# Down, output, key, query and value products as four 32-column strips in one PSUM bank, laid beside the value products of attention

## The chip, the cores and the metric

One core of one Trainium2 chip. The metric is device time in microseconds; every run told of here was in the fast state. The kernel before: 843.19 us, median of 3 runs (843.08 to 843.36). TensorE is called PE here, VectorE DVE and ScalarE ACT, as in the profile.

## The reference, cut to what matters

For 2048 rows of width 512 it adds an attention of 32 heads of 16 to a gated feed-forward of width 1792, with a gate of its own for each row.

```python
q, k, v = qkv[0], qkv[1], qkv[2]                     # x @ wqkv, 32 heads of 16
scores = jnp.einsum("bhqd,bhkd->bhqk", q, k) * (Dh ** -0.5)
p = _softmax(scores, axis=-1)
o = jnp.einsum("bhqk,bhkd->bhqd", p, v)
a = o.transpose(...).reshape(B, S, D) @ wo
b = (_silu(x @ w_gate) * (x @ w_up)) @ w_down
return g * a + (1 - g) * b                           # g = sigmoid(sum(x * gate_w))
```

The softmax has 32 x 2048 x 2048 exponentials: that is the kernel's work. The products are small beside it.

## The kernel before

The program is laid out by a plan that runs when it is built. The plan keeps a foreseen time for PE, DVE and ACT and decides which instruction goes next on each engine. Each turn of the main loop emits a pair of score matmuls (tile s_t, an exponential on ACT follows) and fills PE's room before the next pair with one of: a score block d_t for DVE's own exponential, a value product of attention (o_ps, "pv"), or a piece of side work. DVE's exponentials come in units of four d_t blocks. Side work and d_t share three PSUM banks (`m_tile` takes one, `m_free` gives it back). PE has three forms of instruction: "R", two 64-row halves side by side; "C", four 32-column strips; "F", the full array. The plan counts 0.1 us for each change of form.

Down and output products use `two_banks`: two products run at once in the two row halves, each half adds into its own bank, and after half of the steps they swap halves.

```python
    def two_banks(n, name, a, b, end, stop=True):

        st = {}

        def pc(k):
            v, i = divmod(k, n)

            def f():
                if k == 0:
                    while m_ready(2) is None:
                        stuck()
                    st["a"], st["b"] = m_tile(name + "_a"), m_tile(name + "_b")
                if k == n:
                    sync(ordered(nc.tensor.nop()), st["half"])
                    spend("R", 0.1 if st["seq"] < plan.seq else 1.5)
                for ps, (w, r), h in ((st["a"], a(i), v), (st["b"], b(i), 1 - v)):
                    rows = slice(64 * h, 64 * h + 64)
                    st["half"] = mm(ps[:, :], lhsT=w[rows, :], rhs=r[rows, :], start=(k == i == 0),
                                    stop=(stop and k == 2 * n - 1), tile_position=(64 * h, 0), skip_group_check=True)
                spend("R", 1)
                st["seq"] = plan.seq
                if k == 2 * n - 1:
                    end(st["a"], st["b"])
            return f
        return [(1, pc(k), 2 if k == 0 else 0, "R", st if k == n else None) for k in range(2 * n)]
```

Key, query and value products are in the full form, two steps a piece:

```python
    def k_pieces(b, tb):

        st = {}

        def pc(h):
            def f():
                if h == 0:
                    st["p"] = m_tile("kp")
                    if tb == 0:


                        kst[b] = (on_t[1], bblk)[b == 1][:, :, :].rearrange("p b q -> p (b q)")
                for dc in (2 * h, 2 * h + 1):
                    mm(st["p"][:, :], lhsT=wqk[:, dc, D + P * b:D + P * (b + 1)],
                       rhs=xT[:, dc, tb * QBW:(tb + 1) * QBW], start=(dc == 0), stop=(dc == DC - 1))
                spend("F", 2)
                if h == 1:
                    later(0.6, lambda: end(tb, st["p"]))
            return f
        # ... end(): copy to SBUF, free the bank
        return [(2, pc(0), True), (2, pc(1), False)]

    def down_pieces(qb, tq):

        def rows(t):
            return lambda fc: (mt[:, fc, t * P:(t + 1) * P], wd_t[:, fc, :])

        def done_down(pa, pb):
            for t, p in ((tq, pa), (tq + 1, pb)):
                later(0.65, lambda t=t, p=p: end(t, p))
        # ... end(t, p): scale into bblk, free the bank
        return two_banks(FC, "dps", rows(tq), rows(tq + 1), done_down)
```

The choice in the main loop:

```python
            n_pv = pv_list(plan.pe)
            switch = 0.0 if plan.mode == "C" else 0.1
            fits = int((room + SLACK - switch) / 0.216)
            c = side(room + SLACK)
            if n_pv and fits > 0 and (plan.mode == "C" or len(n_pv) > 1 and fits > 1 and (pv_turn[0] or c is None)
                                      or back >= EB - 4 or c is None and fits == 1):
                emit_pv(n_pv[0])
                pv_turn[0] = False
                continue
            if c is not None:
                put_piece(c)
                pv_turn[0] = True
                continue
            # ... keep-busy strips, or the next pair of scores
```

## Time and profile before

| | before |
|---|---|
| time | 843.19 us |
| ACT busy | 97%: 850 exponentials e_t of 1024 columns, 56 tanh |
| DVE busy | 93%: 87 units of exponentials (348 blocks d_t), all evictions |
| PE matmuls | 5987, changes of form 1052 (counted in the trace) |
| DVE idle, 25 to 820 us | 36.4 us |

The prediction below shows the page's lines, the table of windows, DVE's waits and two pieces of PE's timeline. One habit is needed for all that follows: an ACT instruction that starts late shows as a longer step from start to start, not always as idle time, because two e_t overlap. So I use a ledger: first e_t + 0.904 us for each further e_t + 26.7 us of tanh + a rest = start of the last e_t; after it comes the tail.

### The profile page before, as it was taken

The page shows a single profiled execution, that of the slowest core. Times are in us where ns is not written, and L with a number is a line of the kernel's source. Part 1 is how long each engine was busy: PE and PEld are TensorE (multiplying, and loading weights), DVE is VectorE, ACT ScalarE, POOL GpSimd, SP SyncE. Part 2 cuts the span into 40 slices and gives each one's busy share as a digit, 9 for nine tenths or more (in the row PEclk, how much of TensorE's full clock was granted, in tenths as well). Part 3 has the DMA queues.
Part 4 walks back from the last instruction along what each step waited for, and adds up shares of the span by engine and source line. Part 5 has one row for each costly group of instructions (what it writes and reads, how often), then busy time and mean ns, then how long its engine had stood idle before and what let it go on. Part 6 is the DMA issues. An engine that isn't in the chain of part 4 may idle for free. (4 is left out here: it accounts for less than half of the span.)

```text
span 840.3 us, 16080 instructions
## 1 busy us (share of the span) xinstructions
PE 759.7 (90%) x5987; PEld 260.4 (31%) x6020; DVE 785.5 (93%) x1141; ACT 815.2 (97%) x916; POOL 94.9 (11%) x120
## 2 busy tenths in 40 slices
PE   7899899899989999999899998898999988998986
PEld 3222232233333333233333332222333322332322
DVE  6999998989999989999999899989999999999895
ACT  3999999999999999999999999999999999999996
POOL 5010100100101011110111101010011011000110
PEclk9999999999999999999999999999999999999999
DMA  9432252544455433554445435453544445363240
GB/s 204 128 70 45 57 98 58 108 92 86 96 104 111 92 80 73 108 114 92 99 88 107 80 87 105 92 107 74 104 90 80 91 95 108 89 124 60 58 95 26
DMA packets 101127, 77.18 MB, mean 92 GB/s; under 512 B 77728, under 2 KB 89592, under 8 KB 101048
## 3 DMA queue, kind: packets, MB, share of 16 engines
q0 software_dynamic: 12384, 45.09, 28.7%
q1 hardware_dynamic: 86792, 30.60, 15.5%
q8 instruction: 47, 0.77, 0.4%
q10 hardware_dynamic: 1872, 0.46, 0.2%
q14 instruction: 32, 0.26, 0.1%
HBM read 20.83 MB, written 2.34 MB: 28 GB/s over the span
## 5 line engine op out<-in xcount | busy, mean ns | idle before, releaser
L160 ACT ACTIVATE e_t<-s_t 128x1024 bf16<-128x1024 f32 x850 | 797.0, 1173 | 5.3 <-PE s_t L157 5.2
L157 PE MATMUL s_t<-qx,kaug 64*128 64x512 bf16 x1376 | 279.3, 380 | 51.0 <-ACT e_t L160 44.6
L157 PEld LDWEIGHTS <-kaug 64*128 64x128 bf16 x2048 | 140.3, 93 | 341.4 <-issue 306.5
L166 DVE TENSOR_SCALAR y_t<-d_t 128x512 uint16<-128x512 f32 x348 | 229.0, 682 | 17.9 <-PE d_t L157 15.1
L157 PE MATMUL o_ps<-e_t,vaug 128*32 128x512 bf16 x1700 | 160.0, 389 | 3.0 <-DVE osb L166 2.9
L157 PE MATMUL gu_b<-xT,wu 64*128 64x512 bf16 x440 | 133.1, 375 | 0.4 <-DVE y_t L166 0.2
L157 PE MATMUL gu_a<-xT,wg 64*128 64x512 bf16 x440 | 132.4, 375 | 0.0
L157 PE MATMUL d_t<-qx,kaug 64*128 64x512 bf16 x288 | 105.3, 377 | 4.6 <-DVE y_t L166 1.6
L157 PEld LDWEIGHTS <-vaug 128*32 128x32 bf16 (+1 forms) x2084 | 44.8, 94 | 139.0 <-issue 138.1
L802 POOL DMA_DIRECT2D y_t<-u_t x43 | 40.5, 943 | 356.2 <-PE s_t L157 165.6
L802 POOL DMA_DIRECT2D y_t<-kaug x36 | 36.6, 1016 | 294.8 <-PE s_t L157 141.3
L157 PE MATMUL dps_b<-wd_t,mt 64*128 64x512 bf16 x224 | 65.6, 375 | 0.0
L157 PE MATMUL dps_a<-wd_t,mt 64*128 64x512 bf16 x224 | 65.3, 375 | 0.0
L166 DVE TENSOR_SCALAR z_t<-y_t 128x2048 uint16<-128x2048 uint16 x87 | 60.1, 691 | 2.1
L166 DVE TENSOR_SCALAR y_t<-y_t 128x2048 uint16<-128x2048 uint16 x87 | 59.5, 684 | 1.4 <-DMA y_t<-kaug 1.4
L166 DVE TENSOR_TENSOR u_t<-u_t 128x2048 f16<-128x2048 f16 x43 | 52.6, 1223 | 1.1
L166 DVE TENSOR_TENSOR u_t<-u_t,z_t 128x2048 f16<-128x2048 f16 x43 | 52.3, 1216 | 0.0
L157 PE MATMUL s_t<-q,kaug 64*128 64x512 bf16 x216 | 43.8, 386 | 4.7 <-ACT e_t L160 4.0
L166 DVE TENSOR_TENSOR kaug<-kaug 128x2048 f16<-128x2048 f16 x37 | 45.2, 1222 | 0.9
L157 PEld LDWEIGHTS <-wg 64*128 64x128 bf16 (+1 forms) x444 | 41.2, 94 | 15.6 <-issue 1.8
L157 PEld LDWEIGHTS <-wu 64*128 64x128 bf16 (+1 forms) x444 | 41.3, 94 | 12.7 <-issue 0.9
L166 DVE TENSOR_TENSOR kaug<-kaug,z_t 128x2048 f16<-128x2048 f16 x37 | 45.0, 1215 | 0.0
(136 smaller groups left out, 631.0 us busy)
## 6 DMA issues: line engine op xcount, KB each, us to landing
y_t<-u_t POOLq DMA_DIRECT2D x43, 512.0 KB, 4.9
y_t<-kaug POOLq DMA_DIRECT2D x36, 512.0 KB, 4.9
wg<-in_B_w_gate_dram SPq DMA_DIRECT2D x56, 128.0 KB
wu<-in_B_w_up_dram SPq DMA_DIRECT2D x56, 128.0 KB
y_t<-wd_t POOLq DMA_DIRECT2D x7, 512.0 KB, 4.6
on<-osb SPq DMA_DIRECT2D x120, 16.0 KB
rb<-rr SPq DMA_DIRECT2D x15, 128.0 KB
wd_t<-in_B_w_down_dram SPq DMA_DIRECT2D x7, 256.0 KB
```

The source lines that it names most:

```text
L157: return ordered(nc.tensor.matmul(*args, **kw))
L160: ordered(nc.scalar.activation(*args, **kw))
L166: return lambda *a, **kw: ordered(f(*a, **kw))
L802: nc.gpsimd.dma_start(out=ya, in_=ua, accum_op=ALU.add)
```

## The change

The intent: make the side products in the form of the value products of attention, so that they can lie next to them with no change of form between, and make each in one bank.

```diff
+    def columns(n, name, lhs, rhs, end, c0=0):
+        st = {}
+        def pc(k):
+            def f():
+                if k == 0:
+                    st["p"] = m_tile(name)
+                w, r = lhs(k), rhs(k)
+                for j in range(4):
+                    mm(st["p"][32 * j:32 * j + 32, c0:QBW], lhsT=w[:, 32 * j:32 * j + 32], rhs=r, start=(k == 0),
+                       stop=(k == n - 1), tile_position=(0, 32 * j), skip_group_check=True)
+                spend("C", 1)
+                if k == n - 1:
+                    end(st["p"])
+            return f
+        return [(1, pc(k), k == 0) for k in range(n)]
 # k_pieces, v_pieces, q_pieces, q0_pieces, lone gate and up chains: (cut)
-        return [(2, pc(0), True), (2, pc(1), False)]
+        return columns(DC, "kp", lhs, ..., lambda p: later(0.6, lambda: end(tb, p)))
 # down and output, now one tile of rows a chain: (cut)
-        return two_banks(FC, "dps", rows(tq), rows(tq + 1), done_down)
+        return columns(FC, "dps", ..., lambda p: later(0.65, lambda: end(p)))
-        for tq in range(0, TQ, 2):
+        for tq in range(TQ):
 # planned DVE durations: value copy 0.7 -> 0.54, reciprocal 1.0 -> 0.87,
 # normalisation 0.45 -> 0.345, key maximum 2.6 -> 2.46
-            soon = [c for c in ready if len(c.pieces[c.i]) == 3 and c.deadline <= plan.slot + 4]
-            if len(cur.pieces[cur.i]) > 3 and soon:
+            soon = [c for c in ready if len(c.pieces) <= DC and c.deadline <= plan.slot + 4]
+            if len(cur.pieces) > DC and soon:
-            if n_pv and fits > 0 and (plan.mode == "C" or len(n_pv) > 1 and fits > 1 and (pv_turn[0] or c is None)
-                                      or back >= EB - 4 or c is None and fits == 1):
+            col = c is not None and (c.pieces[c.i][3:] or "C")[0] == "C"
+            visit = len(n_pv) + (len(c.pieces) - c.i if col else 0)
+            if n_pv and fits > 0 and (plan.mode == "C" or visit > 1 and fits > 1 and (pv_turn[0] or c is None or col)
+                                      or back >= EB - 4 or (c is None or col) and fits == 1):
```

`soon` lets a short chain that is almost due interrupt a longer one; `visit` counts the value products and strip steps that could share one change of form.

More of the change, by code (lines that the diff above doesn't have):

```diff
@@ L407, in k_pieces @@
     def k_pieces(b, tb):
-        st = {}
-        def pc(h):
-            def f():
-                if h == 0:
-                    st["p"] = m_tile("kp")
-                    if tb == 0:
-                        kst[b] = (on_t[1], bblk)[b == 1][:, :, :].rearrange("p b q -> p (b q)")
-                for dc in (2 * h, 2 * h + 1):
-                    mm(st["p"][:, :], lhsT=wqk[:, dc, D + P * b:D + P * (b + 1)],
-                       rhs=xT[:, dc, tb * QBW:(tb + 1) * QBW], start=(dc == 0), stop=(dc == DC - 1))
-                spend("F", 2)
-                if h == 1:
-                    later(0.6, lambda: end(tb, st["p"]))
-            return f
         def end(t, p):
@@ L435, in end, with lhs @@
                                           in_=kst[b][DH * hh:DH * (hh + 1), :])
-        return [(2, pc(0), True), (2, pc(1), False)]
+        def lhs(dc):
+            if dc == 0 and tb == 0:
+                kst[b] = (on_t[1], bblk)[b == 1][:, :, :].rearrange("p b q -> p (b q)")
+            return wqk[:, dc, D + P * b:D + P * (b + 1)]
+        return columns(DC, "kp", lhs, lambda dc: xT[:, dc, tb * QBW:(tb + 1) * QBW],
+                       lambda p: later(0.6, lambda: end(tb, p)))
     def k_bound(b):
@@ L454, in v_pieces, with end @@
     def v_pieces(tt):
-        st = {}
-        def pc(h):
-            def f():
-                if h == 0:
-                    st["p"] = m_tile("vp")
-                for dc in (2 * h, 2 * h + 1):
-                    mm(st["p"][:, 64:D], lhsT=xT[:, dc, tt * P:(tt + 1) * P], rhs=wv[:, dc, 64:D],
-                       start=(dc == 0), stop=(dc == DC - 1))
-                spend("F", 2)
-                if h == 1:
-                    later(0.7, end)
-            return f
-        def end():
+        def end(p):
             dst = vaug[:, tt, 4 * VC:G * 4 * VC].rearrange("p (h c) -> p h c", c=VC)[:, :, 1:1 + DH]
-            vec.tensor_copy(out=dst, in_=st["p"][:, 64:D].rearrange("p (h c) -> p h c", c=DH))
-            m_free(st["p"], plan.dve)
-        return [(2, pc(0), True), (2, pc(1), False)]
+            vec.tensor_copy(out=dst, in_=p[:, 64:D].rearrange("p (h c) -> p h c", c=DH))
+            m_free(p, plan.dve)
+        return columns(DC, "vp", lambda dc: xT[:, dc, tt * P:(tt + 1) * P], lambda dc: wv[:, dc, 64:D],
+                       lambda p: later(0.54, lambda: end(p)), c0=64)
     qx = [big.tile([P, 2, 2, QBW], BF16, name=f"qx{i}") for i in range(2)]
@@ L492, in q_pieces, with landed, end @@
     def q_pieces(qb, b):
-        st = {}
-        def pc(h):
-            def f():
-                if h == 0:
-                    st["p"] = m_tile("qp")
-                for dc in (2 * h, 2 * h + 1):
-                    mm(st["p"][:, :], lhsT=wqk[:, dc, P * b:P * (b + 1)],
-                       rhs=xT[:, dc, qb * QBW:(qb + 1) * QBW], start=(dc == 0), stop=(dc == DC - 1))
-                spend("F", 2)
-                if h == 1:
-                    st["c"] = plan.chain
-                    later(0.6, end, key=("q", b))
-            return f
-        def end():
-            me = st["c"]
+        def landed(p):
+            me = plan.chain
+            later(0.6, lambda: end(p, me), key=("q", b))
+        def end(p, me):
             qst = work.tile([P, QBW], BF16, tag="qst", name="qst")
-            vec.tensor_copy(out=qst[:, :], in_=st["p"][:, :])
-            m_free(st["p"], plan.dve)
+            vec.tensor_copy(out=qst[:, :], in_=p[:, :])
+            m_free(p, plan.dve)
             for hh in range(8):
@@ L525, in end @@
             later(0.21, mag, plan.dve, ("q", b))
-        return [(2, pc(0), True), (2, pc(1), False)]
+        return columns(DC, "qp", lambda dc: wqk[:, dc, P * b:P * (b + 1)],
+                       lambda dc: xT[:, dc, qb * QBW:(qb + 1) * QBW], landed)
     def q0_pieces(qb):
         st = {}
-        def pc(h):
-            def f():
-                if h == 0:
-                    st["p"] = m_tile("qp")
-                for dc in (2 * h, 2 * h + 1):
-                    mm(st["p"][:, :], lhsT=wpad[0][:, dc, :], rhs=xT[:, dc, qb * QBW:(qb + 1) * QBW],
-                       start=(dc == 0), stop=(dc == DC - 1))
-                spend("F", 2)
-                if h == 1:
-                    later(1.2, end)
-            return f
-        def end():
+        def end(p):
             for v in range(2):
-                vec.tensor_scalar(out=q0[qb][:, v, :], in0=st["p"][:, :], scalar1=vsel[:, v:v + 1], scalar2=None,
+                vec.tensor_scalar(out=q0[qb][:, v, :], in0=p[:, :], scalar1=vsel[:, v:v + 1], scalar2=None,
                                   op0=ALU.mult)
-            m_free(st["p"], plan.dve)
+            m_free(p, plan.dve)
             aq = mt[:, 4:6, :]
@@ L553, in end, with end_b @@
             st["aq"] = aq
-        def bound():
-            st["b"] = m_tile("bp")
+        def end_b(p):
             for v in range(2):
-                mm(st["b"][:, :], lhsT=kneg0, rhs=st["aq"][:, v, :], start=(v == 0), stop=(v == 1))
-            spend("F", 2)
-            later(1.2, end_b)
-        def end_b():
-            for v in range(2):
-                vec.scalar_tensor_tensor(out=q0[qb][:, v, :], in0=st["b"][:, :], scalar=vsel[:, v:v + 1],
+                vec.scalar_tensor_tensor(out=q0[qb][:, v, :], in0=p[:, :], scalar=vsel[:, v:v + 1],
                                          in1=q0[qb][:, v, :], op0=ALU.mult, op1=ALU.add)
-            m_free(st["b"], plan.dve)
-        return [(2, pc(0), True), (2, pc(1), False)], [(2, bound, True)]
+            m_free(p, plan.dve)
+        return (columns(DC, "qp", lambda dc: wpad[0][:, dc, :], lambda dc: xT[:, dc, qb * QBW:(qb + 1) * QBW],
+                        lambda p: later(1.2, lambda: end(p))),
+                columns(2, "bp", lambda v: kneg0, lambda v: st["aq"][:, v, :], lambda p: later(1.2, lambda: end_b(p))))
     def bound_pieces(qb, b):
@@ L574, in f @@
             st["p"] = m_tile("bp")
-            mm(st["p"][0:8, :], lhsT=kneg[:, b, :], rhs=aqs[(qb, b)][:, :], start=True, stop=True)
-            spend("F", 1)
+            mm(st["p"][0:8, :], lhsT=kneg[:, b, :], rhs=aqs[(qb, b)][:, :], start=True, stop=True,
+               tile_position=(0, 0))
+            spend("C", 1)
             later(0.6, end)
@@ L605, in f @@
             later(0.15, end)
-        return [(0.7, f, True)]
+        return [(0.7, f, True, "F", None)]
     def gate_end():
@@ L658, in gu_chain, with end @@
             return two_banks(DC, "gu", rows(w_gate, i), rows(w_up, i - 1), both)
-        st = {}
         get, end = (rows(w_gate, 0), gate) if i == 0 else (rows(w_up, i - 1), lambda p: later(0.6, lambda: gated(p)))
-        def pc(h):
-            def f():
-                if h == 0:
-                    st["p"] = m_tile("gu")
-                for dc in (2 * h, 2 * h + 1):
-                    w, r = get(dc)
-                    mm(st["p"][:, :], lhsT=w, rhs=r, start=(dc == 0), stop=(dc == DC - 1))
-                spend("F", 2)
-                if h == 1:
-                    end(st["p"])
-            return f
-        return [(2, pc(0), True), (2, pc(1), False)]
+        return columns(DC, "gu", lambda dc: get(dc)[0], lambda dc: get(dc)[1], end)
     scaled = set()
     def down_pieces(qb, tq):
-        def rows(t):
-            return lambda fc: (mt[:, fc, t * P:(t + 1) * P], wd_t[:, fc, :])
-        def done_down(pa, pb):
-            for t, p in ((tq, pa), (tq + 1, pb)):
-                later(0.65, lambda t=t, p=p: end(t, p))
-        def end(t, p):
-            n = qb * TQ + t
+        def end(p):
+            t, n = tq, qb * TQ + tq
             share = omg if qb < QB - 1 else ge
@@ L693, in end @@
             m_free(p, plan.dve)
-        return two_banks(FC, "dps", rows(tq), rows(tq + 1), done_down)
+        return columns(FC, "dps", lambda fc: mt[:, fc, tq * P:(tq + 1) * P], lambda fc: wd_t[:, fc, :],
+                       lambda p: later(0.65, lambda: end(p)))
     e_of = {}
@@ L927, in spread @@
                                   in_=rr[8 * b:8 * b + 8, :].unsqueeze(1).broadcast_to([8, DH, QBW]))
-        at.setdefault(n0 + 6, []).append(lambda: later(1.0, spread))
+        at.setdefault(n0 + 6, []).append(lambda: later(0.87, spread))
         for b in range(g1 // 2):
@@ L932, in norm @@
                 normed.add((qb, b))
-            at.setdefault(n0 + 13 + b, []).append(lambda norm=norm: later(0.45, norm))
+            at.setdefault(n0 + 13 + b, []).append(lambda norm=norm: later(0.345, norm))
     def recip_here(osb):
@@ L978, in fin_pieces, with end @@
     def fin_pieces(qb, tq):
-        def rows(t):
-            return lambda b: (onc[qb][:, b, t * P:(t + 1) * P], wo_t[:, b, :])
-        def done_fin(pa, pb):
-            for t, p in ((tq, pa), (tq + 1, pb)):
-                later(0.67, lambda t=t, p=p: end(t, p))
-        def end(tq, p):
+        def end(p):
             store(qb * TQ + tq, p, bblk[:, tq, :])
             m_free(p, plan.dve)
-        return two_banks(NB, "a_ps", rows(tq), rows(tq + 1), done_fin)
+        return columns(NB, "a_ps", lambda b: onc[qb][:, b, tq * P:(tq + 1) * P], lambda b: wo_t[:, b, :],
+                       lambda p: later(0.67, lambda: end(p)))
     kp0 = [ps_s.tile([P, 2 * QBW], F32, tag="s", name="kp0") for _ in range(2)]
@@ L1092, in bnd @@
                 def bnd(b=b):
-                    later(2.6, lambda: k_bound(b))
+                    later(2.46, lambda: k_bound(b))
                 after = prev = [pace.add([(0.2, bnd, False)], 0, d - 34, ks)]
@@ L1129 @@
             prev = [c]
-        for tq in range(0, TQ, 2):
-            c = pace.add(down_pieces(qb, tq), 0 if qb else 100, a0 + per * (0.6 + 0.3 * (tq + 2) / TQ if qb < QB - 1 else 0.68 + 0.32 * (tq + 2) / TQ), prev + fin_prev + gates)
+        for tq in range(TQ):
+            c = pace.add(down_pieces(qb, tq), 0 if qb else 100, a0 + per * (0.6 + 0.3 * (tq + 1) / TQ if qb < QB - 1 else 0.68 + 0.32 * (tq + 1) / TQ), prev + fin_prev + gates)
             prev = [c]
@@ L1140 @@
             break
-        for tq in range(0, TQ, 2):
+        for tq in range(TQ):
             rel = (UNIT.index((qb, G - 1)) + 1) * KT + 24
-            dl = max(a0 + per * (0.9 + 0.1 * (tq + 2) / TQ), rel + 7 + 3 * tq)
+            dl = max(a0 + per * (0.9 + 0.1 * (tq + 1) / TQ), rel + 7 + 3 * tq)
             def cond(qb=qb):
@@ L1245, in side @@
         mms, _, takes = c.pieces[c.i][:3]
-        mode, two = c.pieces[c.i][3:] or ("F", None)
+        mode, two = c.pieces[c.i][3:] or ("C", None)
         if two and two["seq"] == plan.seq:
```

## The prediction

> **What bounds the kernel now.** I read the head of the page first, then the costliest groups.
>
> ```profile
> PE 759.7 (90%) x5987; PEld 260.4 (31%) x6020; DVE 785.5 (93%) x1141; ACT 815.2 (97%) x916; POOL 94.9 (11%) x120
> ...
> L160 ACT ACTIVATE e_t<-s_t 128x1024 bf16<-128x1024 f32 x850 | 797.0, 1173 | 5.3 <-PE s_t L157 5.2
> ...
> L166 DVE TENSOR_SCALAR y_t<-d_t 128x512 uint16<-128x512 f32 x348 | 229.0, 682 | 17.9 <-PE d_t L157 15.1
> ```
>
> The softmax exponentials are shared out. ScalarE (ACT) takes 850 tiles e_t of 1024 columns, VectorE (DVE) makes the rest by arithmetic, 348 blocks d_t of 512 columns in 87 units of four. ACT waits 5.2 us for a score in the whole run. Since two e_t overlap in the pipeline I also took the starts of successive ACT instructions from the timeline: the median from one e_t to the next is 0.904 us. The ledger up to the start of the last e_t, at 830.6 us: first e_t at 18.7, 849 x 0.904 = 767.5, 56 tanh that together hold ACT for 26.7, and 17.7 left over, of which about 13 are in 66 gaps of 0.96 us or more. After the last start come 9.7 us of tail. So **ACT is the bound, and almost all of the time is the number of e_t.** A change on TensorE (PE) can pay in two ways only: the 13 us of late scores, or units that move from ACT to DVE. One unit moved is two e_t fewer, 1.81 us. On DVE it costs 4 x 0.60 (d_t blocks) + 0.72 + 0.73 + 1.14 + 1.18 + 0.60, start to start in the timeline: 6.8 us. So 1 us of free DVE time is worth 0.27 us of ACT.
>
> Next I looked at who lets DVE idle, and in which stretch. This is the table of windows (us, then busy time of each engine with its instructions); 220 to 260 us is gate and up products, 120 to 200 holds key, query and value products, the others hold the down products.
>
> ```profile
> core 0: us, PE busy (x) PEld busy (x) DVE busy (x) ACT busy (x) POOL busy (x), PEclk, DMA share, GB/s
> 120.00:200.00 80.00, 72.80 (x551) 23.74 (x558) 70.56 (x107) 78.08 (x89) 7.46 (x8) 0.98 0.43 86
> 220.00:260.00 40.00, 36.55 (x297) 12.78 (x296) 39.79 (x58) 40.00 (x48) 3.67 (x5) 1.00 0.53 99
> 280.00:320.00 40.00, 38.35 (x338) 14.69 (x338) 37.21 (x51) 40.00 (x45) 3.75 (x4) 1.00 0.37 76
> 460.00:500.00 40.00, 38.92 (x339) 14.10 (x338) 36.43 (x51) 40.00 (x46) 3.45 (x4) 1.00 0.40 87
> 620.00:660.00 40.00, 38.85 (x336) 14.37 (x333) 38.13 (x52) 40.00 (x46) 4.92 (x5) 1.00 0.34 69
> 780.00:820.00 40.00, 37.19 (x325) 13.17 (x323) 36.31 (x53) 39.61 (x44) 3.75 (x4) 1.00 0.36 74
> ```
>
> DVE is idle 0.2 us in the stretch of gate and up, but 9.4 us in 120 to 200 and 2.8 + 3.6 + 1.9 + 3.7 = 12.0 us in the four of down. The waits of DVE name the releaser:
>
> ```profile
> DVE y_t L166 <- PE d_t L157: 15.1, 22, 1.5
> DVE osb L166 <- PE o_ps L157: 5.9, 3, 5.2
> DVE qst L166 <- PE qp L157: 3.3, 3, 1.6
> ```
>
> Last, PE's timeline where key products run, then where down products run.
>
> ```profile
> 188.37 0.39 PE L157 MATMUL s_t<-qx,kaug 64*128 64x512 bf16 x2
> 188.69 0.61 PE L157 MATMUL kp<-xT,wqk 128*128 128x512 bf16 x2
> 189.29 0.39 PE L157 MATMUL s_t<-qx,kaug 64*128 64x512 bf16 x2
> 189.61 0.40 PE L157 MATMUL o_ps<-e_t,vaug 128*32 128x512 bf16 x4
> 190.20 0.39 PE L157 MATMUL s_t<-qx,kaug 64*128 64x512 bf16 x2 [0.19 <-ACT e_t L160]
> ```
>
> ```profile
> 630.37 0.38 PE L157 MATMUL dps_a<-wd_t,mt 64*128 64x512 bf16 x1
> 630.39 0.38 PE L157 MATMUL dps_b<-wd_t,mt 64*128 64x512 bf16 x1
> ...
> 630.65 0.39 PE L157 MATMUL s_t<-qx,kaug 64*128 64x512 bf16 x2
> ...
> 630.97 0.62 PE L157 MATMUL o_ps<-e_t,vaug 128*32 128x512 bf16 x8
> ```
>
> There are three forms: two 64-row halves side by side (scores, gate and up, down), full 128x128 (key, query, value), and four 32-column strips (value products of attention). A step within a form takes 215 to 227 ns. From scores to full is 308 ns and back 366, from scores to strips 306 and back 357 (medians of the starts). A visit away from the scores so costs about 0.23 us for nothing. I counted 1052 changes of form, 232 of them into or out of the full form.
>
> **What the Trainium skill says.** "TensorEngine Tiling (Array Packing)", Tiling Modes, Key Properties: changing the tiling mode drains the engine, changing the tile alone does not. The trace agrees: 91 to 139 ns more at each change. The same page, Restrictions and Gotchas, Gotcha 1: different row tiles may not be in one PSUM bank at once. That is why down now holds dps_a and dps_b together, two of the three side banks that d_t also needs. "TensorE: Matmul & The Clock Gate", Weight-path perf modes, gives the fast weight load to full 128-column weights only, so strips lose it. The trace shows no price here: a 32-column load takes 94 ns against 97 for a 128-column one, and strip steps follow at 226 and then 216 ns with four loads each. "Perfetto Trace Analysis", Identifying the Most-Contended Engine: occupancy is a fair measure for ScalarE and VectorE, not for PE. So I take ACT's 97% seriously and PE's 90% not.
>
> **The change, part by part.**
>
> 1. Instructions. Counted from the program: down 448 matmuls become 896, output 96 become 192, value 64 and key 64 become 256 each, query 76 become 304, its group-0 bound 6 become 24, the two lone gate and up chains 8 become 32: about 1200 more matmuls and as many loads. Array time does not change: a step of four strips is 0.216 us, as two halves or one full product. All four strips read the same moving tile. The keep-busy strips on xT do this already: four start within 10 ns and the next group comes 209 ns after the last. Cost: 0.
>
> 2. Changes of form. Some 110 visits in the full form go (gates and a few singles stay). 110 x 0.23 = 25 us of PE. Where the new strips do not find a value product to lie beside they need a visit of their own, and down, which now sits among scores with no change at all, needs one too. Down and output are 272 steps; with two steps a visit that is some 140 visits, most of them beside one of the 410 visits that exist. I take 50 new ones, 11 us. Net about 14 us of PE, some 150 changes fewer. None of it is on the path while ACT is fed, apart from the late scores: of their 13 us about 3.5 lie between 100 and 140 us, among key and value products. I credit 1 us.
>
> 3. Banks. Down holds one bank for 14 steps in place of two for 28, so its bank-time halves, and two banks stay for d_t. DVE's idle time in the stretches with rewritten products is 9.4 + 12.0 us, and about 3 more round the output products. I let half of these 24 us be won: 12 us.
>
> 4. Planned durations. The order of instructions is fixed by a plan made ahead, which gives DVE a unit when it foresees time for it. The change lowers four planned costs: 16 x 0.16 + 4 x 0.13 + 15 x 0.105 + 4 x 0.14 = 5.2 us. The trace confirms the new values (0.534 for the value copy, 0.860, 0.334, 2.32 + 0.14), so DVE does nothing faster. The plan only stops leaving 5 us unused.
>
> Sum: 12 + 5.2 = 17 us of DVE for more units, 17 / 6.8 = 2.5, times 1.81 = 4.5 us; with 1 us of late scores, 5.5. Half of a unit is not to be had, and tail and head stay, so I take 5: **843.2 - 5 = 838.2 us.**
>
> **The rivals.** (a) Nothing moves: the count of units hangs on where each unit of work ends in the plan, and DVE's waits may come from PE being full, not from banks. For it: PE is 97% busy in 460 to 500 us. Against: the plan gets 5 us of DVE for certain. Then one unit at most, 841 to 843. (b) New visits hurt: down needs strips where no value product is ready, a visit of value product and two strips is 0.65 + 0.2 plus the score's 0.22, over the 0.904 that ACT leaves, and scores come late. If 60 of the 272 steps cost 0.05 us each, 3 us are lost: 842 to 845. Against: two score buffers, and PE idles 67 us between 25 and 820. (c) Nearly all large DVE gaps close, 27 us over 0.15 us in that stretch, and with the 5 that is nearly five units, 9 us: 834.
>
> **Range and chances.** The central case is two to three units. One unit gives about 841, five 833.5. Neither an unchanged time nor a small loss is excluded. 833 to 842.5 should hold it 8 in 10. Faster by over 2% needs 826, nine units, 61 us of DVE where only 36 are idle in the steady part: 0.02. Slower by over 2% would need a mistake in the plan's order: 0.01.
>
> **What would show it.** Right: e_t falls from 850 to 844 or 846, d_t rises from 348 to 356 or 360, PE has some 7200 matmuls, changes of form fall to about 900 with the full ones nearly gone, strip steps stay at 0.216 us, DVE's wait for d_t falls from 15.1 below 9, and its idle time in the down stretches about halves. Wrong: strip steps over 0.23 us, an e_t count of 850, more gaps over 0.96 us between e_t, or DVE idle at the same places with another releaser.

## The result, and the profile after

836.26 us, median of 4 runs (835.1 to 836.42), against 843.28 us for the kernel before, median of 4 (843.08 to 845.26). The ratio is 0.9909, 95% interval 0.9891 to 0.9926. A ratio is the mean time of one kernel's fast runs over that of the other's of the same rounds, so not quite the ratio of the medians. The class is "same" at the 2% mark, and the gain is real.

The page of the kernel after, the same three lines as the prediction shows of the kernel before:

```profile
PE 776.7 (93%) x7230; PEld 248.0 (30%) x7230; DVE 799.5 (96%) x1168; ACT 810.2 (97%) x910; POOL 102.5 (12%) x123
...
L160 ACT ACTIVATE e_t<-s_t 128x1024 bf16<-128x1024 f32 x844 | 791.7, 1165 | 2.4 <-PE s_t L157 2.2
...
L166 DVE TENSOR_SCALAR y_t<-d_t 128x512 uint16<-128x512 f32 x360 | 233.5, 683 | 1.3 <-PE d_t L157 0.8
```

Three units moved from ACT to DVE (850 to 844 e_t, 348 to 360 d_t), and DVE went from 93 to 96%. DVE's waits (us in total, times, longest) show what gave it the time:

```profile
DVE osb L166 <- PE o_ps L157: 5.1, 2, 2.7
DVE o_t L166 <- PE a_ps L157: 3.9, 3, 2.2
...
DVE y_t L166 <- PE d_t L157: 0.8, 2, 0.5
```

The wait for d_t fell from 15.1 to 0.8 us. The down products begin earlier now, so here is the table of windows of the kernel after over its own four stretches of down (columns as in the prediction):

```profile
254.00:301.00 47.00, 46.19 (x477) 12.59 (x473) 46.37 (x64) 46.98 (x52) 7.89 (x7) 1.00 0.37 74
416.00:466.00 50.00, 49.70 (x514) 13.89 (x506) 49.42 (x70) 50.00 (x56) 7.45 (x7) 1.00 0.36 70
597.00:646.00 49.00, 48.38 (x507) 13.62 (x505) 48.55 (x69) 49.00 (x55) 8.71 (x7) 1.00 0.40 78
766.00:811.00 45.00, 43.41 (x463) 12.24 (x455) 44.48 (x66) 44.88 (x50) 5.11 (x5) 1.00 0.40 83
```

DVE is idle 0.63 + 0.58 + 0.45 + 0.52 = 2.2 us there. In the kernel before it was 10.7 us over its own four (288 to 318, 454 to 488, 626 to 657, 779 to 816 us). PE's timeline shows how strips lie beside the value products:

```profile
98.46 0.40 PE L157 MATMUL o_ps<-e_t,vaug 128*32 128x512 bf16 x4
98.69 0.36 PE L157 MATMUL vp<-rb,xT 128*32 128x448 bf16 x4
98.99 0.39 PE L157 MATMUL s_t<-on,kaug 64*128 64x512 bf16 x2
```

The value projection vp follows the attention product 0.23 us later, the step within a form. Where the kernel before made two visits, with four changes of form, this is one. Yet the changes of form as a whole rose from 1052 to 1279. Those with the full form fell from 232 to 22, as foreseen. But visits for strips rose from 410 to 629, since down and output, which lay among the scores at no cost, now need visits.

The ledger of the two profiled runs, worked out from the starts in the timeline (us):

| | first e_t | 0.904 each | tanh | rest | last e_t | tail | span |
|---|---|---|---|---|---|---|---|
| before | 18.7 | 767.5 | 26.7 | 17.6 | 830.6 | 9.7 | 840.3 |
| after | 19.4 | 762.1 | 26.7 | 15.2 | 823.5 | 11.0 | 834.5 |

5.4 of the 5.8 us between these two runs are the six e_t, 2.4 are scores that come less late, and 2.0 were given back at the start and in the tail.

One thing in the traces must be read beside all this: the granted clock of PE. In the profiled run of the kernel before it is 0.50 for 3.4 us, and in that of the kernel after it is nowhere below 1.00 between 5 and 834 us. The table of windows of the kernel before, that stretch and the 3.4 us ahead of it, then such a pair of the run kqv_full, told of below (PEclk is the third figure from the end):

```profile
126.80:130.20 3.40, 1.97 (x14) 0.49 (x10) 2.43 (x5) 2.70 (x3) 0.86 (x1) 1.00 0.04 7
130.20:133.60 3.40, 3.40 (x14) 0.61 (x13) 1.88 (x4) 2.43 (x3) 0.00 (x0) 0.50 0.84 164
```

```profile
106.40:109.80 3.40, 1.42 (x20) 0.45 (x19) 2.70 (x5) 1.18 (x2) 0.00 (x0) 1.00 0.96 184
109.80:113.20 3.40, 3.40 (x24) 0.61 (x16) 3.37 (x5) 2.61 (x4) 0.00 (x0) 0.50 0.16 28
```

Scores come 2.2 us late in 130 to 134 us alone, so most of the 2.4 us of less late scores are this one stretch. The profiled runs of nine of the fourteen kernels have such stretches before the tail, twelve in all. Each follows 3.4 us in which PE was busy only 19 to 70%, but 56% in the run kqv_alone was followed by none. It matters for the size of the gain too. Beside the experiments the kernel before ran 44 times: the 21 runs with a mean clock of 0.996 or more have a median of 841.7 us, the 18 with 0.994 or less 844.0 us. The four runs of the kernel after had 0.996 to 1.000; the clocks of the four runs of the kernel before that they are compared with are not on record. Against 841.7 us, an estimate of the gain at like clocks is 5.4 us of the 7.0.

### The profile page after: what moved, and what is told of

It reads as the page before. It is cut to its first block, busy times and chain, and to the rows that moved or that the text cites. A ratio compares the mean times of both kernels' runs of the same rounds, so it can differ in the third digit from the quotient of the medians.

```text
span 834.5 us, 18549 instructions
## 1 busy us (share of the span) xinstructions
PE 776.7 (93%) x7230; PEld 248.0 (30%) x7230; DVE 799.5 (96%) x1168; ACT 810.2 (97%) x910; POOL 102.5 (12%) x123
## 5 line engine op out<-in xcount | busy, mean ns | idle before, releaser
L166 DVE TENSOR_SCALAR y_t<-d_t 128x512 uint16<-128x512 f32 x360 | 233.5, 683 | 1.3 <-PE d_t L157 0.8
L157 PEld LDWEIGHTS <-kaug 64*128 64x128 bf16 x2048 | 126.0, 93 | 332.4 <-issue 308.6
L157 PE MATMUL o_ps<-e_t,vaug 128*32 128x512 bf16 x1688 | 167.2, 390 | 2.1 <-DVE osb L166 1.4
L749 POOL DMA_DIRECT2D y_t<-u_t x44 | 46.1, 1047 | 369.7 <-PE s_t L157 217.8
L157 PEld LDWEIGHTS <-vaug 128*32 128x32 bf16 (+1 forms) x2096 | 49.1, 93 | 140.4 <-issue 139.3
L157 PE MATMUL dps<-wd_t,mt 128*32 128x512 bf16 x896 | 77.4, 383 | 0.4 <-DVE bblk L166 0.3
L166 DVE TENSOR_TENSOR u_t<-u_t 128x2048 f16<-128x2048 f16 x45 | 55.0, 1222 | 1.0
L166 DVE TENSOR_TENSOR u_t<-u_t,z_t 128x2048 f16<-128x2048 f16 x45 | 54.8, 1218 | 0.2
L160 ACT ACTIVATE th<-gu_a 128x512 bf16<-128x512 f32 x55 | 41.9, 763 | 0.0
```

Source lines behind the costliest of these rows:

```text
L157: return ordered(nc.tensor.matmul(*args, **kw))
L160: ordered(nc.scalar.activation(*args, **kw))
L166: return lambda *a, **kw: ordered(f(*a, **kw))
L749: nc.gpsimd.dma_start(out=ya, in_=ua, accum_op=ALU.add)
```

## The experiments

Theory (**banks**): DVE gets more units because down and output hold one side bank, not two, so d_t blocks find a bank. Rival (**forms**): what pays is the full-form visits of key, query and value that are gone. Second rival (**durations**): the corrected planned durations do it alone. A third, which was not tested by a run of its own, is the **clock**: stretches of PE at half clock that come or stay away. Twelve kernels ran, in three calls, each on one chip with its own runs of the kernel before; 5 rounds each, all correct. A figure in us that is worked out from two ratios is their difference times 843; it compares runs on different chips, and where the medians in us say something else, both are given. "Idle" is DVE's idle time from 25 to 820 us, "rest" and "tail" are of the ledger of the profiled run.

| label | ratio to before (95%) | e_t | idle | rest | tail |
|---|---|---|---|---|---|
| before | 1 | 850 | 36.4 | 17.6 | 9.7 |
| after | 0.9909 (0.9891 to 0.9926) | 844 | 19.2 | 15.2 | 11.0 |
| down_rows | 0.9931 (0.9918 to 0.9944) | 848 | 30.0 | 14.5 | 9.6 |
| hold2 | 0.9966 (0.9952 to 0.9981) | 850 | 36.3 | 14.0 | 9.6 |
| down_full | 0.9924 (0.9907 to 0.9940) | 846 | 24.6 | 13.7 | 10.2 |
| old_place | 0.9934 (0.9921 to 0.9947) | 844 | 19.2 | 18.2 | 9.5 |
| bank_only | 1.0029 (1.0010 to 1.0048) | 846 | 27.4 | 17.7 | 16.5 |
| consts_only | 0.9994 (0.9972 to 1.0016) | 850 | 37.6 | 16.6 | 9.7 |
| old_consts | 0.9938 (0.9916 to 0.9959) | 848 | 30.4 | 16.6 | 9.5 |
| kqv_full | 1.0083 (1.0060 to 1.0106) | 846 | 32.7 | 23.7 | 16.3 |
| kqv_alone | 0.9953 (0.9936 to 0.9970) | 850 | 37.1 | 14.2 | 9.6 |
| late_ffn | 0.9999 (0.9981 to 1.0017) | 844 | 21.7 | 19.2 | 13.0 |
| gu_cols2 | 0.9916 (0.9893 to 0.9939) | 842 | 14.2 | 15.9 | 13.6 |
| nopre2 | 0.9892 (0.9869 to 0.9915) | 842 | 12.3 | 16.4 | 10.1 |

### down_rows: down and output back in two banks

```diff
 # in the kernel after
-        return columns(FC, "dps", ...)      # and the output products
+        return two_banks(FC, "dps", rows(tq), rows(tq + 1), done_down)
```

> The kernel after, but with the down and output products as before: two of them at a time in 64-row halves, two banks held for 28 steps. Key, query, value in strips, planned durations and placement as changed. Bank theory (the gain is DVE getting d_t blocks because down and output hold one bank and not two): most of the gain goes, the program as built has 848 e_t and 352 d_t (88 units, two fewer than 90), so 3.6 us slower than the kernel after, 839 to 841; DVE idle in the down stretches comes back to about 12 us, in 120 to 200 us it stays under 3. Form theory (the gain is the full-form visits of key, query and value that are gone): the gain stays, 836 to 837, since those are still strips.

Measured 836.41 us against 841.86 for before on that chip, ratio 0.9931. Both theories were too sure: in us the form theory's 836 to 837 was met, by the ratio the run lies between the two, and its interval overlaps that of the kernel after. DVE's idle time in the down stretches came back (15.6 us over 255 to 287, 416 to 451, 593 to 627 and 760 to 814 us) and two units were lost, as banks say. But 5.8 us of the gain stayed (0.0069 of 843), and the one unit that is left is 1.8 of them, so something else pays too, which banks did not foresee; kqv_alone below looks at it alone.

### hold2: strips, but a second bank is held and not used

```diff
+                if two and "h" not in st:        # two=True for down and output
+                    t = m_ready()
+                    if t is not None and t <= plan.pe:
+                        st["h"] = min((i for i in range(3) if banks[i] is not None), key=lambda i: banks[i])
+                        banks[st["h"]] = None
```

> The kernel after with one thing undone: each down and output chain takes a second side bank in the plan, as soon as one is free, and leaves it unused until it ends. Same matmuls, same strips. Bank theory: the gain of this part goes, the program as built has 850 e_t and 348 d_t, so 840 to 843. Form theory: strips are as before, changes of form stay at about 1270 against 1279, so 836 to 837.

Ratio 0.9966: 4.8 us slower than the kernel after by the ratios (0.0057 of 843), 2.6 us by the medians (838.9 against 836.26), with the same strips and 1277 changes of form against 1279. Three units were lost. The first two down stretches of hold2 in the table of windows:

```profile
253.00:296.00 43.00, 42.76 (x450) 11.36 (x448) 36.53 (x50) 42.99 (x48) 4.61 (x5) 1.00 0.35 69
417.00:460.00 43.00, 43.00 (x461) 11.42 (x453) 38.02 (x53) 43.00 (x48) 3.93 (x5) 1.00 0.35 69
```

DVE is idle 6.5 and 5.0 us there, 22.8 us over all four, and waits 18.8 us for d_t in all; its idle time from 25 to 820 us is that of the kernel before (36.3 against 36.4 us). This is the cleanest proof of the bank: the matmuls of a down product are the same, only a bank that nobody uses is missing.

### down_full: one bank, without strips

```diff
-        return columns(FC, "dps", ...)      # and the output products
+        return full(FC, "dps", ...)         # one 128-column matmul a step, spend("F", 1)
```

> The kernel after with down and output products in the full 128-column form, one product in one bank, one step a piece, where the kernel after has four strips. It has the one bank without the strips. Bank theory: nearly all of the gain stays, built with 846 e_t and 356 d_t, 837 to 839. Form theory (strips beside value products are what helps): falls back towards 841 to 843, because each visit has two changes of form of its own.

Ratio 0.9924, 846 e_t: not told apart from the kernel after. DVE is idle 3.8 us in its down stretches. For down and output the bank is what counts; no gain from their strips shows.

### old_place: value products are placed by the old rule

```diff
-            if n_pv and fits > 0 and (plan.mode == "C" or visit > 1 and fits > 1 and (pv_turn[0] or c is None or col)
-                                      or back >= EB - 4 or (c is None or col) and fits == 1):
+            if n_pv and fits > 0 and (plan.mode == "C" or len(n_pv) > 1 and fits > 1 and (pv_turn[0] or c is None)
+                                      or back >= EB - 4 or c is None and fits == 1):
```

> The kernel after, but the rule that picks the moment for value products of attention is the one of before: it no longer goes first when a strip chain is waiting. If the placing next to value products is what pays: 838 or more, with more changes of form. If banks and planned durations pay: built with the same 844 e_t and 360 d_t, so 836 +- 1, and about as many changes of form (1247 in the plan against 1274).

Ratio 0.9934, 844 e_t, 1252 changes of form: about as many. Strips come to lie beside value products under either rule. It is nominally 0.0025 behind the kernel after, with 3.0 us more rest in the profiled run, but the intervals overlap. More than these 3.0 us lie in a stretch of half clock: in 805.5 to 812.3 us the granted clock is 0.50 and the scores come 4.2 us late. So what the rule is worth, between nothing and some 2 us, stays open.

### bank_only: the bank alone, on the kernel before

```diff
 # in the kernel before
-        return two_banks(FC, "dps", ...)    # and the output products
+        return full(FC, "dps", ...)         # one product, one bank, full form
```

> The kernel before with one part alone: down and output products are made one at a time in one side bank, in the full 128-column form, one step a piece. No strips anywhere, old planned durations, key, query, value as before. Bank theory: this part alone brings two of the three units, built with 846 e_t and 356 d_t, 3.6 us and a little more off: ratio to before 0.995 +- 0.0015. DVE idle in the four down stretches falls from 12 us to under 5, and its wait for d_t from 15 to under 10. Form theory: more changes of form than before (down left the scores' form), so no gain or a loss, ratio 1.000 or over.

Ratio 1.0029: slower than before, as the form theory had it (1298 changes of form against 1052), and the bank theory's ratio failed. Yet each step of the bank theory came true but the last: 846 e_t, DVE idle in the down stretches 3.9 us and not 10.7, last e_t at 827.1 and not 830.6. The scores come no later than before (rest 17.7 against 17.6): the loss is in the tail, 16.5 us in place of 9.7. Its timeline on PE at the end, and the wait of ACT for the last product:

```profile
826.52 0.39 PE L157 MATMUL s_t<-qx,kaug 64*128 64x512 bf16 x2
...
827.39 4.49 PE L157 MATMUL dps<-wd_t,mt 128*128 128x512 bf16 x20
...
831.82 0.39 PE L157 MATMUL a_l_a<-wo_t,on 64*128 64x512 bf16 x1
```

```profile
ACT mt L160 <- PE a_l_b L157: 10.7, 1, 10.7
```

The last score is out, and 20 steps of down are still to do: 4.5 us of PE with nothing beside them. The first three down stretches take 48 to 53 us here, where two products at once took some 30 to 37. They begin at 288 us as before, and the last, from 798 us, still runs at 831.5. **Total PE time does lie on the path, at the end.** down_full has the same down products and ends well (tail 10.2), and its down begins at 253 us. That the early beginning is the reason is argued from this pair and from kqv_full; the two differ in key, query and value products and planned durations as well.

### consts_only: the planned durations alone

```diff
 # in the kernel before
-            later(0.7, end)     # 1.0 spread, 0.45 norm, 2.6 k_bound
+            later(0.54, end)    # 0.87,       0.345,     2.46
```

> The kernel before with the four planned durations of the change alone (value copy, reciprocal, normalisation, key maximum). If the planned durations were worth the 5.2 us of DVE time that the prediction gave them by themselves, one unit more: 848 e_t, ratio 0.998. As built it has 850 e_t, the same 87 units, so I expect a ratio of 1.000 +- 0.001: without a free bank the plan cannot use the time.

Ratio 0.9994 with an interval over 1, no unit moved. The second rival falls: durations do not do it alone.

### old_consts: the kernel after with the old planned durations

```diff
 # in the kernel after
-                       lambda p: later(0.54, ...)   # 0.87, 0.345, 2.46
+                       lambda p: later(0.7, ...)    # 1.0,  0.45,  2.6
```

> The kernel after with the four planned durations of before. Built with 848 e_t (88 units, two fewer than after). If the number of e_t sets the time, 3.6 us slower than the kernel after: ratio to before 0.995. If forms and banks do by themselves and the planned durations do not matter: 0.991 as after.

Ratio 0.9938, 848 e_t: two units fewer, nominally 2.4 us slower than the kernel after, though the intervals overlap. DVE's idle time falls only from 36.4 to 30.4 us. With consts_only it says that the durations gave no unit alone and go with two where the banks are free. One unit either way can also come from a plan that falls out differently, so I do not size it closer.

### kqv_full: key, query, value in the full form again

```diff
 # in the kernel after
-        return columns(DC, "kp", ...)       # kp, vp, qp, bp
+        return full(DC, "kp", ...)          # one 128-column matmul a step, spend("F", 1)
```

> The kernel after with key, query, value and bound products in the full 128-column form, still one step a piece; down and output in strips. Built with 846 e_t (89 units). Counting e_t alone gives 1.8 us over the kernel after, ratio 0.993. Form theory (the full-form visits are what cost): most of the gain goes, 0.997 or more, and the long gaps between e_t in 100 to 140 us come back to over 3 us. If the pieces of one step are what removed those gaps, they stay under 1.5 us here.

Ratio 1.0083: the form theory's forecast of 0.997 or more was right, and the e_t count was wrong by 13 us. With two units more than before it is 7 us slower than before. Long gaps between e_t came back: 3.9 and 1.8 us over the median step in 100 to 120 and 120 to 140 us (0.4 and 0.2 in the kernel after), and the tail is 16.3 us, for the same reason as in bank_only: gate and up products begin at 154.7 us (117.9 in the kernel after), down at 289, and the last down eviction starts at 837.6 us. How the form does it is not shown, though: three stretches of half clock (24.5 to 31.3, 109.8 to 113.2 and 782.2 to 785.7 us) hold 9.1 us of late scores, and the whole rest is 8.5 us over that of the kernel after.

### kqv_alone: strips for key, query and value alone

```diff
 # in the kernel after
-        return columns(FC, "dps", ...)      # down, output: back to two_banks
+        return two_banks(FC, "dps", ...)
-            later(0.87, spread)             # and the other three planned durations
+            later(1.0, spread)
```

> Key, query and value products in strips alone: down and output in two banks and the planned durations as before. Built with 850 e_t, as many as before. If only the number of e_t sets the time: ratio to before 1.000. If strips make key, query and value cheaper for PE where scores are late, the long gaps between e_t in 100 to 140 us go (3.6 us before, 0.6 after) and the gate and up products begin near 118 us and not near 155: ratio 0.996 +- 0.0015, with no unit moved.

Ratio 0.9953, with 850 e_t as before: 4.0 us (0.0047 of 843) with no unit moved, as forecast. The rest falls from 17.6 to 14.2 us; the excess in 100 to 140 us from 3.6 to 0.8. Gate and up begin at 126.4 us and not 155.2. Beside the strips this kernel keeps the pieces of one step, the placing rule and the `soon` rule of the kernel after; kqv_full, which has these too, was slow, so the form is needed. Two ways in which it pays are mixed: fewer and shorter visits, and a PE that is granted more clock. The nine runs have a mean clock of 0.998, the 22 of before beside them 0.994. A straight line through the 44 runs of before gives 0.56 us more for each 0.001 of clock less (correlation -0.91), so an estimate is that 2 of the 4 us go with the clock. Whether strips keep the clock up, or only went with it, no run separates.

### late_ffn: the early start taken away

```diff
-            c = pace.add(pcs, 58, a0 + ...)
+            c = pace.add(pcs, 85, a0 + ...)
```

> The kernel after with one number changed: gate and up products may not begin before slot 85 (in the kernel after, slot 58), so near 155 us as in the kernel before and not near 118. Built with 844 e_t as after. If the early start that strips give is what lets the one-bank down products end in time, the last down eviction comes late (829 us or more, as in the two slow kernels bank_only and kqv_full), the tail after the last e_t grows from 11 to about 16 us and the ratio is 0.996 or more. If the early start is idle time merely moved: 0.991 as after, tail 10 to 11 us.

Ratio 0.9999: all of the gain is gone, but only in part for the reason I gave. The last down eviction starts at 828.1 us, near the forecast, yet the tail grew to 13.0 and not 16. The larger loss is one I had not thought of. With gate and up out of the way, key products ran early and met a transfer:

```profile
137.39 0.69 DVE L166 CAST on<-kp 128x512 bf16<-128x512 f32 x1 [3.79 <-DMA kaug<-on]
...
140.20 1.02 ACT L160 ACTIVATE e_t<-s_t 128x1024 bf16<-128x1024 f32 x1 [3.44 <-PE s_t L157]
```

The key copy waits 3.8 us until its buffer has been read out, and ACT then stands still for 3.4 us; PE, busy for only 0.64 us of the 3.4 us up to 139.0 us, is granted half clock in the next 3.4 us. So this run does not tell cleanly what the early start is worth; it shows only that a late start lengthens the tail by about 2 us. The pair bank_only and down_full is the better evidence.

### gu_cols2: the same for gate and up products

```diff
-            return two_banks(DC, "gu", rows(w_gate, i), rows(w_up, i - 1), both)
+            return (columns(DC, "gu", ...up..., lambda p: later(0.6, lambda: gated(p)))
+                    + columns(DC, "gu", ...gate..., gate))
```

> The change carried on: gate and up products too are made one at a time, in four strips in one bank, where the kernel after makes two at a time in 64-row halves in two banks. Built with 842 e_t (91 units, one more than after), 1594 changes of form in the plan against 1274. If banks and e_t count: ratio to before 0.989. If PE's changes of form have become the limit: 0.995 or more, with longer gaps between e_t or a longer tail.

Ratio 0.9916: no better than the kernel after. The unit came (842 e_t) and DVE's idle time fell to 14.2 us, but changes of form rose to 1598 and the tail to 13.6 us (the last down eviction starts at 823.4 us). Both expected effects are there and cancel.

### nopre2: a chain that holds two banks is not interrupted

```diff
-            soon = [c for c in ready if len(c.pieces) <= DC and c.deadline <= plan.slot + 4]
+            soon = [c for c in ready if len(c.pieces) <= DC
+                    and c.deadline <= plan.slot + (4 if cur.pieces[0][2] != 2 else -2)]
```

> The kernel after, but a short chain no longer breaks into a gate and up chain that holds two banks, unless it is two slots overdue. In the kernel after, output products break in at 520 and 700 us, the three side banks are all held and DVE idles 5.3 and 3.9 us there. Built with 842 e_t (91 units). If that is bank starvation: DVE idle at 520 and 700 us under 2 us together, ratio 0.989. If not, DVE idles there all the same, ratio 0.991.

This one came from reading the kernel after: DVE idles 5.3 us in 520 to 540 us. PE's timeline there, d_t, gate and output products only:

```profile
520.49 0.38 PE L157 MATMUL d_t<-qx,kaug 64*128 64x512 bf16 x1
523.09 0.39 PE L157 MATMUL a_ps<-wo_t,on 128*32 128x512 bf16 x4
...
525.52 0.38 PE L157 MATMUL gu_a<-xT,wg 64*128 64x512 bf16 x1
...
529.31 0.38 PE L157 MATMUL gu_a<-xT,wg 64*128 64x512 bf16 x1
...
531.05 0.38 PE L157 MATMUL d_t<-qx,kaug 64*128 64x512 bf16 x1
```

A gate and up chain is under way with two banks, the output chain breaks in and takes the third, and for 10.6 us there is no d_t. The table of windows for 520 to 540 us, the kernel after, then nopre2:

```profile
520.00:540.00 20.00, 18.08 (x173) 5.57 (x172) 14.70 (x21) 20.00 (x24) 0.86 (x1) 1.00 0.35 87
```

```profile
520.00:540.00 20.00, 19.12 (x172) 6.50 (x170) 19.83 (x29) 20.00 (x24) 2.58 (x3) 1.00 0.47 100
```

DVE's idle time there goes from 5.3 to 0.2 us, and from 3.9 to 0.2 us in 700 to 720 us; one more unit moves, and the ratio is 0.9892: 834.13 us, with every run (833.14 to 834.76) below the fastest of the kernel after, though that was on another chip. It beats the kernel before and is nominally 1.4 us ahead of the kernel after, with intervals that overlap.

## Why the prediction was right or wrong

The total was right: 838.2 us foretold, 836.26 measured, inside 833 to 842.5. The main path, banks to d_t blocks to units to fewer e_t, was right: three units where two to three were foretold. That the sum came so near is in part luck: late scores gave 2.4 us in the profiled runs and not 1, start and tail, which were to stay, took 2.0, and changes of form went the other way than foretold. By its own steps:

1. **Instructions at no cost: right.** 7230 matmuls were recorded (7200 foretold). A down step of four strips follows the last after 226 ns (median), as a full step of down does in down_full (226 ns); the two halves of before followed after 215 ns.
2. **Changes of form: wrong in number, and wrong in what they are worth.** Foretold: some 150 fewer, about 900, none on the path but 1 us of late scores. Measured: 227 more, 1279. The term that failed is "I take 50 new ones": the strip visits grew by 219. And the late scores were worth more than 1 us: kqv_alone gives 4.0 us with no unit moved. The prediction put 3.5 us of late scores, from 100 to 140 us, among key and value products; 2.2 us of them lie in the stretch of half clock, which its own table shows as PEclk 0.98 in 120 to 200 us and which it passes over. The step "none of it is on the path while ACT is fed" fails at the end of the run: where side work begins late it runs past the last score (bank_only, kqv_full). Gate and up begin 37 us sooner in the kernel after (155.2 to 117.9 us), 29 us sooner with the strips of key, query and value as in kqv_alone (126.4 us), and one-bank down, slower by half, seems to need that.
3. **Banks: right in mechanism, and with the durations right in size.** 12 + 5.2 = 17 us of DVE time foretold, 36.4 - 19.2 = 17.2 us measured over 25 to 820 us; the wait for d_t was to fall below 9 and fell to 0.8. hold2 shows it. The bank-time of down did not halve: two banks over 131 us of stretches became one bank over 192 us, about a quarter less. And the bank alone would have lost (bank_only).
4. **Planned durations: half right.** "The plan gets 5 us of DVE for certain" is wrong: consts_only moved no unit. In the kernel after, putting them back costs two units and 11.2 us of the 17.2; yet bank_only moved two units with the old ones. So the durations gave nothing without a free bank and between nothing and two units with it, and the two terms do not simply add up as in the prediction.

Of the rivals, (a) was wrong, since DVE's waits did come from banks and not from a full PE: in 416 to 466 us PE is busy 49.70 of 50 us and DVE 49.42. (b) did not happen: scores came less late in the kernel after, and no later in gu_cols2 (rest 15.9) and bank_only (17.7) than before (17.6); what those two lost is in the tail. (c) came half way: DVE's gaps over 0.15 us fell from 27.7 to 11.7 us, three units and not five.

Shown by runs: the bank (hold2, down_full), that the strips of key, query and value pay (kqv_alone, kqv_full), the spilling tail (bank_only). Open: how those strips pay, by fewer visits or by fewer stretches of half clock, what the placing rule is worth, how much of old_consts is the plan's own scatter, and the price of a late start by itself (late_ffn is mixed with the stall on the transfer).

## What to carry to other kernels

Where a tuned kernel shares work between two engines, price every change as "how much of the helper's time does it free", and look for buffers that keep the helper from being fed: one bank held idle cost 2.6 to 4.8 us here. An engine that is not the bound still has a bill to pay by the end of the run; before slowing its side work, see when that work ends. And try parts together as well as alone: the bank alone lost 0.3%, the strips of key, query and value alone won 0.5%, both with the rest won 0.9%. Last, read the granted clock stretch by stretch before giving late work a cause: here one stretch of 3.4 us at half clock held 2.2 of the 3.6 us of late scores between 100 and 140 us.

## What the Trainium skill lacked or had wrong

- "TensorEngine Tiling (Array Packing)", Key Properties, says that a change of tiling mode drains the engine but gives no price. In the kernel before a change costs 91 to 139 ns over a step within a form (306 to 308 ns from scores to strips or to the full form, 357 and 366 ns back, against 215 to 227 ns).
- The same page's When to Use Tiling proposes column tiling where the stationary side has 64 columns or fewer. It has no word on splitting a full 128-column product into four strips to stay in the mode of its neighbours: that cost nothing per step of down here (226 ns for strips in the kernel after and for the full form in down_full), and the kernel with such strips for key, query and value ran 0.47% faster (kqv_alone).
- The same page, Restrictions, says that column tiling disables the fast weight load, and "TensorE: Matmul & The Clock Gate", Weight-path perf modes, gives it to full 128-column weights only. With 448 to 512 moving columns no run here shows a price: PE's weight loads were busy 31% of the span before and 30% after, with 7230 loads in place of 6020.
- "TensorEngine Tiling (Array Packing)", Gotcha 1, says that row tiling raises PSUM pressure; it could say what that costs a kernel whose other engines need the banks: 2.6 to 4.8 us of 839 in hold2, where one bank is held and not used.
